# First layer of tiles 3 and 4 one by one from the same sixteen weight buffers, second layer for both; the other tiles in groups of two, two and three

## The chip, the core and the metric

The kernel runs on one core of a Trainium2 chip. The metric is the device time of one execution in microseconds (us). Before the change it took 667.05 us, the median of three runs (666.74 to 670.57).

## What is computed

Attention that keeps the 32 largest scores of each row, then two feed-forward layers. Everything is float32.

```
scores = scale * q @ k.T                     # 2 batches x 8 heads x 576 x 576, head_dim 64
kth = 32nd largest of each row
attn = softmax(where(scores >= kth, scores, -1e9))
x = (attn @ v) of all heads side by side     # 1152 tokens x 512
h = x @ w_in;  g = max(h, 0) + log1p(exp(-|h|));         x = g @ w_out     # 512 -> 2048 -> 512
h = x @ w_in2; g = max(h, 0) + alpha * min(h, 0);   result = g @ w_out2    # 512 -> 2048 -> 512
```

## The kernel before

The 1152 tokens are nine tiles of 128. Attention works on one tile and one head at a time, 72 rows of work in the order of `rows`: tiles 3, 4, 5, 6, 7, 8, 0, 1, 2. For each row TensorE makes the scores (`pss`, L454), ScalarE copies them out (`s`, L459), VectorE finds the 32 largest with four MAX8 and three MATCH_REPLACE8 (L463, L466), ScalarE and GpSimd build the masked exponentials (`e`: L492, L497, L499), TensorE turns them round (`pp`, `pq`: L512, L518), ScalarE copies that (`pt`), and TensorE multiplies by v (`pav`, L540). After the eighth head of a tile, `pr` (L587) spreads the reciprocal sums and the tile's `x` is ready.

The feed-forward part works on groups of tiles (`CHUNKS`, L34): tiles 3 and 4, then 5, 6 and 7, then 8, 0, 1 and 2. For a group, each layer runs over 16 slices `j` of the 2048 hidden columns: `up(j)` makes 128 hidden columns in `ph` (four matrix products of 128 by 128 weights with all tokens of the group), ScalarE and VectorE apply the activation (`g`), `down(j)` multiplies `g` by the output weights into `pa`. The weights of two slices make a unit of 128 x 1024; a layer has 8 units for `up` and 8 for `down`, so both layers have 32.

- The weights come as 64-bit numbers. The first group to need a unit converts it (`convert`): two DMAs into `cr` (one of two buffers, `RAWB`), VectorE L336 and L339, ScalarE L342 twice, GpSimd L345 four times into `cx`, one of the `RING` = 12 buffers called `wring`; a DMA then writes it to scratch memory in DRAM (`ws`).
- The first group (`NATIVE`) multiplies in plain float32, straight from `cx`. The profile shows such a product as two records.
- The other groups fetch the unit from scratch (`w`) and split it (`fetch`): ScalarE casts it to the high part `wh` (L376), GpSimd or VectorE subtracts to get the low part (two halves, `low_piece`, L355 or L356). `x` and `g` are split in the same way (`xh`, `xl`, `gh`, `gl`; `gh` is ScalarE's L662). A product is then three faster matrix products (`three`, L607 to L609).
- In the last group's first layer `down` is turned: the weights are the stationary operand and `g` streams (L608 `pa<-gh,w` is that form's order of names).

The order of all work on all engines is written out by hand in `ORDER`: numbers are operations, a `b` picks the second engine of an operation that has two (VectorE in `low_piece`), and `fN` puts N idle products on TensorE (`scrap`, L766; each one float32 product of 128 x 128, two records in the profile). There are 333 of these. Every engine runs its instructions strictly in this order, so whatever stands behind a waiting instruction on an engine waits with it.

## Time and profile before

| | us | share of the span |
|---|---|---|
| median of three runs | 667.05 | |
| the profiled execution's own time | 665.57 | |
| its span | 663.8 | |
| TensorE (PE) busy | 650.0 | 98% |
| weight loads (PEld) busy | 505.3 | 76% |
| VectorE (DVE) busy | 526.0 | 79% |
| ScalarE (ACT) busy | 487.3 | 73% |
| GpSimd (POOL) busy | 392.6 | 59% |

All times below are from this one profiled execution. Its own time is 1.8 us more than its span, and 1.5 us less than the median of the runs. PE's busy time contains the 333 idle products. A duration given for one instruction reaches a little into the next one of its engine, so rows that follow one another start closer together than their durations say; where that matters, the start-to-start distance is used. [...]

### The profile page before, as it was taken

To read this page: it belongs to the slowest core of one execution; us is meant where nothing else is said; L and a number is where in the kernel's file an instruction comes from. 1 tells how busy PE (TensorE), PEld (TensorE's weight loads), DVE (VectorE), ACT (ScalarE), POOL (GpSimd) and SP (SyncE) were. 2 spreads that over 40 slices of the span, in tenths; PEclk is the share of its full clock that TensorE was granted. 3 is DMA by queue.
4 is the path that set the end of the run, shared out by engine and by line. 5 is a ranking of instruction groups with operands and counts; after the bars stand their busy time and mean duration, and the time that the engine had idled before them with its cause. 6 is when DMAs were issued, how large, how long until landed. Compare 5 with 4: busy or idle time off the path is not lost.

```text
span 663.8 us, 12012 instructions
## 1 busy us (share of the span) xinstructions
PE 650.0 (98%) x4246; PEld 505.3 (76%) x4246; DVE 526.0 (79%) x1003; ACT 487.3 (73%) x1017; POOL 392.6 (59%) x418
## 2 busy tenths in 40 slices
PE   9999999899999999999999999999999999999997
PEld 7789987666656656578887788888888888888885
DVE  4999999999999999999999999899442436434332
ACT  3777777999999888999899886677774647534331
POOL 1466566556875789877878868778632324433310
PEclk9999999999999999999999999999999999999999
DMA  8657466466677688633323112232432223212301
GB/s 294 238 165 244 153 205 227 152 205 192 210 233 240 222 275 265 193 135 112 120 96 112 64 59 76 90 96 64 135 136 95 91 71 125 96 63 98 125 0 63
DMA packets 29579, 96.85 MB, mean 146 GB/s; under 512 B 3408, under 2 KB 3920, under 8 KB 29520
## 3 DMA queue, kind: packets, MB, share of 16 engines
q1 hardware_dynamic: 29520, 96.10, 44.1%
q8 instruction: 33, 0.54, 0.3%
q14 instruction: 26, 0.21, 0.1%
HBM read 76.95 MB, written 19.14 MB: 145 GB/s over the span
## 4 chain that ended last, share of the span: by engine, by line
PE 86%; POOL 4%; ACT 3%; issue 3%; DVE 2%; DMA 1%; SPq 0%; POOLq 0%
PE ph L607 8%; PE pa L607 8%; PE ph L635 8%; PE scrap L766 8%; PE ph L608 8%; PE ph L609 8%; PE pa L609 8%; PE pa L608 8%; PE pa L681 7%; PE pss L454 6%; PE pp L512 4%; POOL cx L345 2%; POOL e L497 2%; DMA cr<-in_w_dram 1%; PE pav__1557 L540 1%
## 5 line engine op out<-in xcount | busy, mean ns | idle before, releaser
L355 POOL TENSOR_TENSOR w<-w,wh 128x512 fp32r<-128x512 f32 x93 | 137.9, 1498 | 110.5 <-ACT wh L376 108.1
L463 DVE MAX8 m<-r 128x8 f32<-128x576 f32 x216 | 155.8, 747 | 0.1
L497 POOL TENSOR_TENSOR e<-s,e 128x288 f32<-128x288 f32 x144 | 120.8, 858 | 56.1 <-ACT e L492 46.2
L345 POOL TENSOR_TENSOR cx<-cx,cr 128x256 int32<-128x256 int32 x128 | 95.1, 766 | 42.3 <-ACT cr L342 38.4
L466 DVE MATCH_REPLACE8 r<-m,r 128x576 f32<-128x576 f32 x144 | 106.2, 741 | 0.0
L342 ACT ACTIVATE cr<-cr 128x512 int16<-128x512 uint32 x64 | 83.8, 1384 | 3.5 <-DVE cr L339 3.4
L766 PEld LDWEIGHTS scrap<-ident 128*128 128x128 f32 x666 | 78.7, 195 | 9.6 <-issue 8.2
L766 PE MATMUL scrap<-ident 128*128 128x128 f32 x666 | 84.0, 282 | 1.4 <-POOL ident masks.py:199 1.4
L376 ACT CAST wh<-w 128x1024 fp32r<-128x1024 f32 x64 | 66.8, 1046 | 15.6 <-DMA w<-ws 14.2
L459 ACT COPY s<-pss 128x288 f32<-128x288 f32 x144 | 53.3, 408 | 24.3 <-PE pss L454 23.6
L607 PE MATMUL pa<-w,gh 128*128 128x512 f32 x160 | 66.6, 416 | 0.0
L463 DVE MAX8 m<-s 128x8 f32<-128x576 f32 x72 | 52.8, 748 | 15.5 <-ACT s L459 14.4
L681 PE MATMUL pa<-cx,g 128*128 128x512 f32 x128 | 63.6, 605 | 0.9 <-POOL cx L345 0.9
L609 PE MATMUL pa<-wh,gh 128*128 128x512 f32 x160 | 63.2, 395 | 0.0
L608 PE MATMUL pa<-wh,gl 128*128 128x512 f32 x160 | 63.1, 395 | 0.0
L499 ACT ACTIVATE e<-e,nb 128x576 f32<-128x576 f32 x72 | 55.7, 774 | 9.9 <-POOL e L497 9.7
L662 ACT CAST gh<-g 128x384 fp32r<-128x384 f32 (+1 forms) x64 | 35.9, 564 | 30.4 <-PE pa L609 19.8
L454 PE MATMUL pss<-ks,q 64*64 64x288 f32 x576 | 51.8, 428 | 2.3 <-ACT pt L515 1.6
L356 DVE TENSOR_TENSOR w<-w,wh 128x512 fp32r<-128x512 f32 x35 | 29.8, 857 | 30.1 <-ACT wh L376 29.9
L466 DVE MATCH_REPLACE8 r<-m,s 128x576 f32<-128x576 f32 x72 | 53.2, 741 | 0.0
L356 DVE TENSOR_TENSOR gl<-g,gh 128x512 fp32r<-128x512 f32 (+1 forms) x36 | 27.5, 764 | 30.9 <-ACT gh L662 30.9
L515 ACT COPY pt<-pp 128x512 f32<-128x512 f32 x72 | 41.5, 587 | 11.2 <-PE pp L512 10.9
(126 smaller groups left out, 1383.0 us busy)
## 6 DMA issues: line engine op xcount, KB each, us to landing
cr<-in_w_dram SPq DMA_DIRECT2D x64, 512.0 KB, 5.3
w<-ws SPq DMA_DIRECT2D x64, 512.0 KB, 3.3
ws<-cx SPq DMA_DIRECT2D x32, 512.0 KB, 6.3
v<-in_v_dram SPq DMA_DIRECT2D x12, 320.0 KB, 6.6
ks<-in_k_dram SPq DMA_DIRECT2D x11, 288.0 KB, 4.3
out_dram<-o SPq DMA_DIRECT2D x9, 256.0 KB, 2.0
q<-in_q_dram SPq DMA_DIRECT2D x8, 256.0 KB, 4.5
ks<-in_k_dram SPq DMA_DIRECT2D x2, 144.0 KB, 2.9
```

Source lines behind the costliest of these rows:

```text
L342: op("ACT", lambda r=r: nc.scalar.activation(r().bitcast(I16)[:, :, 2], r()[:, :, 0], AF.Copy, scale=2.0 ** -29), reads=[part], writes=[r])
L345: op("POOL", lambda part=part, r=r, cs=cs: nc.gpsimd.tensor_add(part().bitcast(I32)[:, cs], part().bitcast(I32)[:, cs], r().bitcast(I32)[: ...
L355: lambda: nc.gpsimd.tensor_sub(lo(), x(), hi().bitcast(F32)),
L454: nc.tensor.matmul(pss[n]()[part], qr()[head, pair, part], ks()[head, cs], start=True, stop=True)
L463: op("DVE", lambda: nc.vector.max(out=out(), in_=x()), reads=reads, writes=writes)
L466: op("DVE", lambda: nc.vector.match_replace(out=out(), in_to_replace=found(), in_values=x(), imm_value=LOWEST), reads=reads, writes=writes)
L497: op("POOL", lambda cs=cs: nc.gpsimd.tensor_sub(e()[:, cs], s()[:, cs], e()[:, cs]), reads=[s], writes=[e])
L607: nc.tensor.matmul(acc, ah, b_l, start=first, stop=False)
L608: nc.tensor.matmul(acc, a_l, bh, start=False, stop=False)
L609: nc.tensor.matmul(acc, ah, bh, start=False, stop=last)
L681: nc.tensor.matmul(acc(), gh()[:, cs], w[0]().bitcast(F32), start=first, stop=last)
L766: plan.emit(ORDER, lambda: nc.tensor.matmul(scrap()[:, :P], ident, ident, start=True, stop=True))
```

## The change

`CHUNKS` becomes five groups: tile 3; tile 4; tiles 5 and 6; tiles 7 and 8; tiles 0, 1 and 2. `TOGETHER` says that the groups of tile 3 and of tile 4 share their second layer, so this layer runs once for 256 tokens, as before. `NATIVE` keeps plain float32 for exactly these two tiles. `RING` goes from 12 to 16 buffers. `lies` remembers which unit lies in which buffer, and `fetch` returns at once where a float32 group finds its unit still there: tile 4's first layer uses the 16 buffers that tile 3's first layer converted. `HOLD` would start a layer at another slice; it is 0 here and moves nothing. `ORDER` is written anew, with 227 idle products instead of 333.

```diff
--- before.py
+++ after.py
@@ -31,8 +31,8 @@
 LOWEST = -3.0e38
 STEEP = 2.0 ** 80
 
-CHUNKS = [[3, 4], [5, 6, 7], [8, 0, 1, 2]]
-TOGETHER = [[0], [1], [2]]
+CHUNKS = [[3], [4], [5, 6], [7, 8], [0, 1, 2]]
+TOGETHER = [[0, 1], [2], [3], [4]]
 SB = 8
 RB = 2
 EB = 2
@@ -46,8 +46,9 @@
 LEAD = 4
 ULEAD = 2
 RAWB = 2
-RING = 12
-NATIVE = {(1, 0), (0, 0)}
+RING = 16
+NATIVE = {(0, 1), (1, 1), (0, 0)}
+HOLD = {(0, 1): 0}
 
 
 class Buffer:
@@ -148,135 +149,157 @@
 
 
 ORDER = """
...
 """
 
 
@@ -320,13 +343,17 @@
     units = [(layer, j, m) for layer in (0, 1) for j in range(FJ // GROUP) for m in (0, 1)]
     ready, scratch = {}, {}
 
-    def slot(tag, bufs, dtype, name):
-        return Halves(buf(tag, bufs, [P, WIDE], dtype, name))
+    lies = {}
+
+    def slot(tag, bufs, dtype, name, unit=None):
+        x = Halves(buf(tag, bufs, [P, WIDE], dtype, name))
+        lies[x.whole.key] = unit
+        return x
 
     def convert(unit):
         layer, j, m = unit
         nm = f"{layer}{m}{j}"
-        f = slot("wring", RING, U32, f"cx{nm}")
+        f = slot("wring", RING, U32, f"cx{nm}", unit)
         raw = Halves(buf("craw", RAWB, [P, WIDE, 2], U32, f"cr{nm}"))
         source = mats[layer][m][j].bitcast(U32)
         for part in raw.parts:
@@ -362,10 +389,12 @@
 
     def fetch(unit, no, ci, whole):
         fresh = unit not in scratch
+        if whole and unit in ready and lies.get(ready[unit][0].whole.key) == unit:
+            return
         if fresh:
             x = convert(unit)
         else:
-            x = slot("wring", RING, F32R, f"w{no}")
+            x = slot("wring", RING, F32R, f"w{no}", unit)
             op("SP", lambda: nc.sync.dma_start(x().bitcast(F32), scratch[unit]),
                reads=["ws%d%d%d" % (unit[0], unit[2], unit[1])], writes=x.parts)
         ready[unit] = (x,)
@@ -622,11 +651,11 @@
             self.turned = layer == 0 and ci == len(CHUNKS) - 1 and len(among[ci]) == 1 and not self.native
             self.g = {}
 
-        def up(self, j):
+        def up(self, j, at):
             n, nm, ci = self.n, f"{self.layer}{self.ci}_{j}", self.ci
             w = [x.parts[j % GROUP] for x in ready[self.layer, j // GROUP, 0]]
             hp = bank("ph", 2, n, f"ph{nm}")
-            step = 1 if j == 0 and self.x[0] is not self.x[-1] else 2
+            step = 1 if at == 0 and self.x[0] is not self.x[-1] else 2
             for c0 in range(0, KT, step):
                 def products(c0=c0):
                     for c in range(c0, c0 + step):
@@ -663,11 +692,11 @@
             low_part(gl, g, gh, n, [g, gh], [gl])
             self.g[j] = gh, gl
 
-        def down(self, j):
+        def down(self, j, at):
             nm, ci = f"{self.layer}{self.ci}", self.ci
             parts_of_g = self.g.pop(j)
             gh, gl = parts_of_g[0], parts_of_g[-1]
-            first, last = j == 0, j == FJ - 1
+            first, last = at == 0, at == FJ - 1
             w = [x.parts[j % GROUP] for x in ready[self.layer, j // GROUP, 1]]
             parts = KT if self.turned else len(self.tiles)
             if first:
@@ -752,14 +781,16 @@
             lay = Layer(layer, ci)
             for j in range(-ULEAD, FJ):
                 if j + ULEAD < FJ:
-                    if (j + ULEAD) % GROUP == 0:
-                        fetch((layer, (j + ULEAD) // GROUP, 0), no, ci, lay.native)
-                    lay.up(j + ULEAD)
+                    n = (j + ULEAD + HOLD.get((layer, ci), 0)) % FJ
+                    if n % GROUP == 0:
+                        fetch((layer, n // GROUP, 0), no, ci, lay.native)
+                    lay.up(n, j + ULEAD)
                     no += 1
                 if j >= 0:
-                    if j % GROUP == 0:
-                        fetch((layer, j // GROUP, 1), no, ci, lay.native)
-                    lay.down(j)
+                    n = (j + HOLD.get((layer, ci), 0)) % FJ
+                    if n % GROUP == 0:
+                        fetch((layer, n // GROUP, 1), no, ci, lay.native)
+                    lay.down(n, j)
                     no += 1
 
     with tc.manual_schedule():
```

The counts in the sections below are of the instructions in program order. A float32 product counts there once, where the profile has two records. What the new order looks like at three places follows; names are those of the code with a running number, and the rows of the changed kernel have its own line numbers.

TensorE from the point where tile 3's attention is done (`pr`), before the change. `scrap` are idle products, `pq` and `pp` turn attention rows round.

```order
L587 MATMUL pr__908<-ident,rx_885 128x128 x4
L766 MATMUL scrap<-ident 128x128 x15
L518 MATMUL pq_943<-ident,e_71 128x128
L512 MATMUL pp_945<-ident,e_71 128x128 x4
L766 MATMUL scrap<-ident 128x128 x7
L540 MATMUL pav__971<-pt_73,v_180 64x64 x10
L540 MATMUL pav__971<-pt_73,v_163 64x64 x10
L766 MATMUL scrap<-ident 128x128 x2
L512 MATMUL pp_1009<-ident,e_72 128x128 x4
L766 MATMUL scrap<-ident 128x128 x15
```

The same place after the change.

```order
L616 MATMUL pr__874<-ident,rx_785 128x128 x4
L797 MATMUL scrap<-ident 128x128 x10
L541 MATMUL pp_906<-ident,e_71 128x128 x4
L797 MATMUL scrap<-ident 128x128 x2
L664 MATMUL ph_1_918<-xh_911,cx_218 128x128 x4
L664 MATMUL ph_0_925<-xh_911,cx_218 128x128 x4
L547 MATMUL pq_939<-ident,e_71 128x128
L541 MATMUL pp_941<-ident,e_71 128x128 x4
L569 MATMUL pav__956<-pt_73,v_167 64x64 x10
L569 MATMUL pav__956<-pt_73,v_171 64x64 x10
L664 MATMUL ph_3_987<-xh_911,cx_272 128x128 x4
L664 MATMUL ph_2_998<-xh_911,cx_272 128x128 x4
```

Behind `pr` stood idle products alone between the attention rows of tile 4; now the first layer of tile 3 (`ph` with 128 columns, weights `cx`) begins there.

TensorE after the change, where the first layer of tile 4 begins. `xh_911` is tile 3's input in the rows above, `xh_1582` is tile 4's; `py` belongs to the end of tile 3's first layer.

```order
L710 MATMUL pa_1024<-cx_1523,g_15_1532 128x512
L664 MATMUL ph_0_1594<-xh_1582,cx_218 128x128 x4
L664 MATMUL ph_1_1607<-xh_1582,cx_218 128x128 x2
L590 MATMUL py_1614<-ident,o_1603 128x128 x4
L664 MATMUL ph_1_1607<-xh_1582,cx_218 128x128 x2
L483 MATMUL pss_1626<-ks_867,q_372 64x288 x2
L483 MATMUL pss_1629<-ks_867,q_372 64x288 x2
L569 MATMUL pav__1639<-pt_73,v_171 64x128 x10
L664 MATMUL ph_2_1658<-xh_1582,cx_272 128x128 x4
L483 MATMUL pss_1669<-ks_867,q_372 64x288 x2
L483 MATMUL pss_1672<-ks_867,q_372 64x288 x2
L710 MATMUL pa_1680<-cx_392,g_0_1612 128x512
```

Tile 4's products name the same buffers `cx_218` and `cx_272` as tile 3's; no conversion and no DMA stands between. The queue of DMAs has no fetch (`w<-ws`) for tile 4: 96 fetches in all, 32 for each of the three later groups, where there were 64.

TensorE where the first three-product layer begins, before the change (tiles 5, 6 and 7) and after it (tiles 5 and 6).

```order
L512 MATMUL pp_3115<-ident,e_71 128x128 x4
L518 MATMUL pq_3120<-ident,e_71 128x128
L607 MATMUL ph_0_3122<-xl_2050,wh_2645 128x384
L608 MATMUL ph_0_3122<-xh_2040,w_2546 128x384
L609 MATMUL ph_0_3122<-xh_2040,wh_2645 128x384
L607 MATMUL ph_0_3122<-xl_2050,wh_2645 128x384
L608 MATMUL ph_0_3122<-xh_2040,w_2546 128x384
```

```order
L541 MATMUL pp_2909<-ident,e_72 128x128 x4
L636 MATMUL ph_0_2919<-xl_2185,wh_2364 128x256
L637 MATMUL ph_0_2919<-xh_2175,w_2291 128x256
L638 MATMUL ph_0_2919<-xh_2175,wh_2364 128x256
L636 MATMUL ph_0_2919<-xl_2185,wh_2364 128x256
L637 MATMUL ph_0_2919<-xh_2175,w_2291 128x256
L638 MATMUL ph_0_2919<-xh_2175,wh_2364 128x256
```

The moving side of a product shrinks from 384 to 256 columns; the number of weight loads for each slice stays at twelve.

## Rows read from the trace of the kernel before

**Rows 1.** Busy time by stretch: columns are stretch, us, then each engine (instructions).

```profile
core 0: us, PE busy (x) PEld busy (x) DVE busy (x) ACT busy (x) POOL busy (x), PEclk, DMA share, GB/s
0.00:54.00 54.00, 52.64 (x480) 44.17 (x481) 44.59 (x89) 36.26 (x78) 22.90 (x36) 1.00 0.71 235
54.00:102.00 48.00, 46.51 (x487) 43.00 (x486) 46.68 (x93) 36.10 (x77) 30.82 (x40) 1.00 0.61 200
152.00:210.00 58.00, 57.42 (x347) 36.56 (x348) 57.55 (x116) 55.94 (x126) 42.39 (x53) 1.00 0.68 219
266.00:317.00 51.00, 48.89 (x332) 35.83 (x331) 49.27 (x101) 47.07 (x110) 40.30 (x43) 1.00 0.47 149
0.00:473.00 473.00, 463.20 (x3426) 354.70 (x3427) 448.16 (x900) 393.29 (x875) 334.15 (x385) 1.00 0.52 169
473.00:663.80 190.80, 186.85 (x823) 150.62 (x821) 77.81 (x104) 93.97 (x142) 58.49 (x34) 1.00 0.26 88
```

**Rows 2.** The last attention rows' transposes on PE: ns min/median/max, first and last start.

```profile
L512 PE MATMUL pp<-ident,e x32: 270/272/273, 440.8 to 473.0; 128*128 128x128 f32 x32
```

**Rows 3.** PE in order of time (start us, us): eleven products of 384, 34 of 512.

```profile
286.28 0.34 PE L608 MATMUL ph<-xh,w 128*128 128x384 f32 x1
...
288.05 0.34 PE L609 MATMUL ph<-xh,wh 128*128 128x384 f32 x1
...
519.22 0.39 PE L608 MATMUL ph<-xh,w 128*128 128x512 f32 x1
...
526.87 0.40 PE L608 MATMUL pa<-gh,w 128*128 128x512 f32 x1
```

**Rows 4.** Chain that ended last, in order of time: start us, us, what, records.

```profile
19.93 5.33 PE scrap L766 x46
...
136.14 0.87 PE pp L512 x8
...
137.88 0.86 PE ph L635 x4
```

**Rows 5.** Groups by form, weight loads: count, busy us, mean ns, idle before.

```profile
L766 PEld LDWEIGHTS scrap<-ident 128*128 128x128 f32 x666 | 78.7, 195 | 9.6 <-issue 8.2 <-POOL ident masks.py:199 1.4
```

**Rows 6.** Groups by form, VectorE.

```profile
L356 DVE TENSOR_TENSOR w<-w,wh 128x512 fp32r<-128x512 f32 x35 | 29.8, 857 | 30.1 <-ACT wh L376 29.9
L655 DVE SCALAR_TENSOR_TENSOR g<-g,rest,ph 128x384 f32<-128x384 f32 x16 | 9.6, 600 | 0.2 <-ACT g L653 0.2
L649 DVE SCALAR_TENSOR_TENSOR g<-ph,g 128x384 f32<-128x384 f32 x16 | 8.7, 543 | 1.1 <-ACT g L648 0.9 <-ACT kb L491 0.3
L655 DVE SCALAR_TENSOR_TENSOR g<-g,rest,ph 128x256 f32<-128x256 f32 x16 | 7.4, 464 | 0.1
L649 DVE SCALAR_TENSOR_TENSOR g<-ph,g 128x256 f32<-128x256 f32 x16 | 6.6, 413 | 0.0
```

**Rows 7.** Groups by form, ScalarE.

```profile
L342 ACT ACTIVATE cr<-cr 128x512 int16<-128x512 uint32 x64 | 83.8, 1384 | 3.5 <-DVE cr L339 3.4
L376 ACT CAST wh<-w 128x1024 fp32r<-128x1024 f32 x64 | 66.8, 1046 | 15.6 <-DMA w<-ws 14.2 <-PE ph L635 1.5
L647 ACT ACTIVATE g<-g 128x384 f32<-128x384 f32 x16 | 8.5, 530 | 0.1
L653 ACT ACTIVATE g<-ph 128x384 f32<-128x384 f32 x16 | 7.8, 488 | 5.4 <-PE ph L609 5.4
L647 ACT ACTIVATE g<-g 128x256 f32<-128x256 f32 x16 | 6.9, 432 | 0.1
L653 ACT ACTIVATE g<-ph 128x256 f32<-128x256 f32 x16 | 6.1, 390 | 0.9 <-PE ph L635 0.8
```

**Rows 8.** ScalarE in order of time: start us, us, instruction.

```profile
162.53 0.48 ACT L647 ACTIVATE g<-g 128x256 f32<-128x256 f32 x1
162.91 0.58 ACT L515 COPY pt<-pp 128x512 f32<-128x512 f32 x1
```

**Rows 9.** Groups by form, GpSimd.

```profile
L355 POOL TENSOR_TENSOR w<-w,wh 128x512 fp32r<-128x512 f32 x93 | 137.9, 1498 | 110.5 <-ACT wh L376 108.1 <-issue 2.3
```

More of the change, by code (lines that the diff above doesn't have):

```diff
@@ new lines @@
+2924 2496 2946 2521 2925b 2856 2911 2872 2533 2873 2857 2494 2534 2956 2858 2910 2878 2933 2859b 2879 2495
+2871 2890 2535 2880 2511 2935b 2934 2947 2891 2881 2888 2970 2536 2949b 2896 2512 2948 2882 2889 2892 2883b
+2957 2509 2897 2510 2537 2902 2893 2982 2959b 2894 2903 2522 2527 2958b 2904 2971 2538 2914 2895b 2915 2973
+2972b 2912 3002 2916 2913 2523 2983 2920 2905 2921 2917 2906 2984b 2985 2918 2926 2524 3014 2907b 2927 2539
+2525 2919 2928 2938 2545 2526 3003 2540 2929 2542 2937 2546 2547 2930 3004b 2541 2950 3005 2543 2945 2931b
@@ new lines @@
+3100b 3101 3040 3050 3142 3041 3052 3042 3054 3043 3131 3053 3044 3133b 3132 3070 3045b 3055 3064 3162 3056
+3062 3143 3065 3057 3082 3145b 3144 3085 3058 3084 3059 3071 3051 3072 3063 3073 3083 3060 3174 3163 3086
+3061b 3074 3164b 3087 3165 3075 3096 3194 3076 3097 3088 3077b 3094 3089 3095 3090 3102 3091 3206 3175 3115
+3092 3116 3176b 3177 3117 3093b 3118 3195 3103 3196b 3197 3114 3104 3129 3207 3119 3105 3209b 3208 3126 3106
+3226 3120 3127 3107 3121 3128 3108 3134 3246 3122 3109b 3123 3135 3124 3125b 3148 3136 3150 3137 3138 3151
@@ new lines @@
+3227 3139 3160 3140 3228b 3264 3229 3152 3149 3141b 3247 3146 3161 3153 3249 3147 3154 3248b 3166 3180 3167
+3155 3156 3158 3265 3157b 3159 3178 3168 3274 3266b 3267 3182 3169 3170 3183 3171 3172 3181 3290 3184 3173b
+3190 3185 3198 3186 3187 3193 3199 3275 3192 3276b 3277 3200 3179 3201 3191 3188 3214 3202 3300 3189b 3291
+3203 3215 3204 3292b 3293 3212 3205b 3316 3216 3210 3217 3211 3218 3213 3219 3225 3220 3222 3221b 3223 3301
+3224 3230 3302b 3326 3303 3232 3234 3317 3236 3238 3231 3318b 3319 3242 3235 3239 3233 3240 3243 3237 3241
@@ L280 @@
+3422b 3423 3356 3348 3360 3349 3431 3350 3372 3432b 3446 3433 3361 3351b 3373 3358 3374 3362 3383 3375 3363
+3385 3364b 3386 3447 3398 3387 3449b 3448 3399 3388 3392 3400 3367 3401 3384 3393 3365 3382 3376 3424 3377b
+3389 3390b 3410 3409 3391 3408 3402 3425 3403b 3411 3426 3427 3412 3418 3413 3417 3414 3415 3434 3416b 3437
+3419 3435 3428 3438 3429b 3444 3439 3451 3440 3436 3443 3441 3445 3442b 3452 3454 3450 3459 3458 3463 3453
+3455 3457 3456 3462 3461 3460 3464
 """
```

125 lines of the change are left out of this document (54 added, 71 removed), and 135 rows, old and new, of the table ORDER.

## The prediction

> **What bounds the kernel now.** I read the busy times by stretch first, then the last attention rows on PE, then PE's instructions in order of time. The last transposes of an attention row start at 473.0 us [rows 2], and that splits the span. Up to there PE (463.2 of 473.0 us) and VectorE (448.2) are both nearly full, ScalarE is at 393.3 and GpSimd at 334.2; behind it PE alone is full, 186.9 of 190.8 us, and the others stand below half [rows 1]. So the end is the time at which attention is through, plus the feed-forward work that PE has left by then. PE's fullness up to 473 us is partly sham: 333 idle products stand there. 46 of their records take 5.33 us [rows 4], 0.116 us each, two for a product: 333 x 0.232 = 77 us.
>
> Distances on PE, start to start: 384 columns (286.28 to 288.05, ten steps) 0.177 us; 512 columns (519.22 to 526.87, 33 steps) 0.232 us [rows 3]. A float32 record of 256 columns takes 0.86 / 4 = 0.215 us [rows 4].
>
> **PE, behind the last attention row.** Before, 795 three-product matmuls of 512 columns stand there in program order: 184.4 us, which with the attention's last pieces and 2% of waits makes the 190.8. After, 180 of 512, 576 of 384 and 30 of 256 columns: 41.8 + 102.0 + 3.7 = 147.5 us. No row shows 256 columns in this form. The line through 384 and 512 falls 0.055 us for each 128 columns, to 0.122. The bounds are 0.116, the pace of the idle products, each of which has a weight load of its own that lasts 195 ns [rows 5] and still keeps that pace, and 0.177, if the pace of 384 is a floor. I take 0.122, since the idle products show that loads follow each other that closely. The tail loses 184.4 - 147.5 = **37 us**: 190.8 becomes 153.8.
>
> **PE, up to the last attention row.** In the same counts 384 matmuls of 384 columns go (-68.0), 738 of 256 come (+90.0), and 87 more of 512 (+20.2). Tiles 3 and 4 one by one turn 64 float32 products of 256 columns into 128 of 128: 64 x 2 x 0.215 = 27.5 us become 128 x 2 x 0.116 = 29.7, the idle product's own shape (+2.2). Four more transposes `py` at 0.109 [rows 4] add 0.4. Together +44.8 us of work, and 106 idle products less give back 106 x 0.232 = 24.6. Net +20 us: with the idle time that PE had, 473 becomes **493**.
>
> **VectorE in the same part.** By program order it gets 13 more weight halves at 0.857 us (+11.1), 24 more pieces L655 of 256 at 0.464 and 14 less of 384 at 0.600 (+2.7), and of L649 32 of 128 (0.283 by the line through 0.413 and 0.543), 16 more of 256, 16 less of 384 (+7.0) [rows 6]. The low parts `gl`, 15 of 256 for 3 of 384 at L649's prices, add 4.5; six masks that go to ScalarE (0.74 by that line) take 4.4. That is 20.9 us in 61 more instructions. Instructions that follow each other start about 0.1 us before the one ahead ends (162.53 + 0.48 against 162.91) [rows 8], so 15 us remain: 448.2 + 15 + the 24.8 it was idle = **488**.
>
> **ScalarE in the same part.** The 32 added unit splits cost 32 casts of 1.046 us (+33.5). Smaller groups mean more pieces: L647 and L648 get 64 of 128 columns at 0.334 (by the line through 0.432 and 0.530; +21.4), 32 more of 256 (+13.8) and 32 less of 384 (-17.0); L646 and L653 32 of 128 at 0.292 (+9.3), 44 more of 256 (+17.2) and 31 less of 384 (-15.1) [rows 7]. The `gh` casts, 60 of 256 for 29 of 384 at L647's prices, add 10.4; six masks and four copies about 7. That is 80.5 us in 188 more instructions, less 0.1 us each: 62 us, so 455. After the first 54 us, in which ScalarE cannot be filled (36.3 us), 419 us are left for it. The fullest stretch of before ran it at 55.94 of 58 us, 96%, with VectorE at 99% and PE at 99%; another, with waits on it, at 47.07 of 51, 92% [rows 1]. At 96% attention ends at 54 + 435 = 489, at 92% at 54 + 454 = 508. The point where ScalarE is tightest is tile 4's attention (54 to 102 us): it had 36.1 us of 48 there, and gets the casts of eight conversions where there were five (6 x 1.384 = +8.3) [rows 7] and 39 pieces of tile 3's first layer (about +9), 53 us in all, so this stretch grows to about 55.
>
> **GpSimd and DMA.** 44 more halves at 1.498 us [rows 9] make 66 us, so 400 of about 495, covered by the same stretch; if it were late, the three products that need the low half would wait, and with them every attention transpose behind on PE. 32 fetches of 512 KB more are 17 MB in about 400 us, beside a DMA share of 0.52 before 473 us [rows 1]; the 16 buffers give a fetch four more to run ahead into. I cost them at nothing; that would fail only if a fetch stood behind a late conversion on the one queue. Tile 4 fetches nothing.
>
> **Sum.** PE says 493, VectorE 488, ScalarE 489 to 508. They are different queues of one order, and each wait of one is felt by the others; I take 495, a little behind the latest of the best cases. 495 + 153.8 = 648.8, 15.0 us under the span of 663.8; taken off the median of 667.05 (the profiled execution itself took 665.57) that is **652 us**.
>
> **Rivals.**
> *ScalarE becomes the bound.* Attention then ends at 508: 508 + 153.8 = 661.8, or 665 for the median. For it: three engines at 94% and more at once, which before held for one stretch only, and conversions that must run through two `cr` buffers faster than before in 54 to 102. Against it: those 58 us show that it can be done. It eats the whole gain at 510 us, that is with ScalarE under 92%.
> *Weight loads set the pace of the short products.* Slower. Twelve loads of 128 x 128 stand before twelve products of 256 columns for each slice, 768 products in all. If their distance stays at 0.177, they cost 768 x 0.055 = 42 us more: 694. The gain is gone from 0.122 + 15 / 768 = 0.142. Against it: the idle products' 0.116. [...]
> *Nothing waits more than before, and VectorE alone sets the pace.* 488 + 153.8 = 641.8: 645. It needs PE to lose some of its 10 idle us.
> *PE's clock falls.* Tile 5's attention loses all idle products and has about 40 us of work in 53. The granted clock was 1.00 throughout, in 54 to 102 with idle products filling [rows 1]. [...]
> *The buffers are not kept* is excluded: the new order names the same `cx` buffers and no fetch.
>
> **Chances.** Forecast, 646 to 660 us: 0.55. ScalarE bound, 660 to 670: 0.2. VectorE alone, 642 to 646: 0.12. Weight loads, 690 and more: 0.06. Clock or something else, 670 to 690: 0.07. About 1%, 6.7 us, is what a measurement can tell from no change: faster than 660.4 is the forecast, the VectorE case and a little of ScalarE's, 0.68; within 1% nearly all of the rest of ScalarE's, 0.2; slower 0.12. The range of 643 to 668 leaves out the lower end of VectorE's case and all above 668, about 0.17.
>
> **What would show it.** Last transposes on PE at 490 to 500 us; a tail of about 154 us; steps of 0.12 us between products of 256 columns; about 454 records of `scrap`; ScalarE at 94% up to the last row; granted clock 1.00. Wrong would make it above all: ScalarE under 92% before the last row, or a step above 0.142.

## The result and the profile after

The changed kernel takes **675.08 us** (median of 7 runs, 672.56 to 679.16), the kernel before 667.33 (7 runs). The ratio is 1.0118, 95% interval 1.0085 to 1.0152: about 1.2% slower, where 652 us and a gain of 2.3% were forecast. The profiled execution took 674.34 us, with a span of 672.6. In the table of runs below, the ratios leave out one slow execution each of one_input and short_topk, and the medians include them.

The last attention row on TensorE splits this span as it split the one before [rows 2] (ns min/median/max, first and last start):

```profile
L541 PE MATMUL pp<-ident,e x32: 270/272/273, 474.6 to 520.4; 128*128 128x128 f32 x32
```

Attention is through at 520.4 us; 495 was forecast, and 473.0 it was before. What stands behind is 672.6 - 520.4 = 152.2 us, forecast 153.8, before 190.8. So the tail came out as worked out, and the whole miss (25 us at the last row) lies ahead of that row. The stretches of [rows 1], now of the changed kernel:

```profile
core 0: us, PE busy (x) PEld busy (x) DVE busy (x) ACT busy (x) POOL busy (x), PEclk, DMA share, GB/s
54.00:102.00 48.00, 45.18 (x425) 34.92 (x424) 48.00 (x104) 43.69 (x105) 32.33 (x43) 1.00 0.68 226
152.00:210.00 58.00, 51.43 (x348) 33.57 (x347) 56.64 (x119) 52.73 (x131) 42.53 (x53) 1.00 0.72 229
266.00:317.00 51.00, 51.00 (x380) 40.66 (x379) 45.30 (x95) 48.20 (x121) 43.55 (x46) 1.00 0.52 167
0.00:520.00 520.00, 492.11 (x3783) 379.67 (x3784) 486.42 (x969) 448.09 (x1060) 402.25 (x446) 0.99 0.57 187
520.00:672.60 152.60, 148.60 (x817) 139.85 (x816) 77.89 (x112) 84.00 (x148) 56.99 (x34) 1.00 0.33 109
```

Up to the last row TensorE is busy for 492.1 us and idle for 27.9, where it was idle for 9.8 before [rows 1]. VectorE is busy for 486.4, ScalarE for 448.1, GpSimd for 402.3. No engine is full from end to end.

Where the attention part lost its time shows in two more views. First, when the float32 products of tiles 3 and 4 run (`xh` is their first layer, `yh` the second). Of the kernel before:

```profile
L635 PE MATMUL ph<-xh,cx x128: 379/379/483, 120.3 to 193.5; 128*128 128x256 f32 x128
L635 PE MATMUL ph<-yh,cx x128: 379/379/483, 203.7 to 268.4; 128*128 128x256 f32 x128
```

Of the changed kernel:

```profile
L664 PE MATMUL ph<-xh,cx x256: 272/275/421, 75.7 to 187.8; 128*128 128x128 f32 x128
L664 PE MATMUL ph<-yh,cx x128: 379/379/634, 195.2 to 261.1; 128*128 128x256 f32 x128
```

Tile 3 alone starts its first layer 44.6 us earlier, and all that is left of it at the end of the second layer is 7.3 us. Second, the exponentials of the attention rows (two records a row) in the kernel before, up to the end of those products and behind it:

```profile
core 0: us, ACT busy (x), PEclk, DMA share, GB/s
0.00:120.30 120.30, 14.48 (x34) 1.00 0.66 218
120.30:268.80 148.50, 19.82 (x46) 1.00 0.68 219
268.80:473.00 204.20, 27.70 (x64) 1.00 0.32 104
```

and in the changed kernel:

```profile
0.00:75.70 75.70, 8.14 (x19) 1.00 0.69 229
75.70:261.50 185.80, 22.61 (x54) 0.98 0.73 235
261.50:520.00 258.50, 31.22 (x72) 0.99 0.43 139
```

Before, 80 records, 40 rows, are through at 268.8 us, 6.7 us a row; now 73 records, 36.5 rows, at 261.5, 7.2 us a row. Behind that a row takes 204.2 / 32 = 6.4 us before and 258.5 / 36 = 7.2 now. The second figure had to rise, since the feed-forward work taken out of the tail stands there. The first had not: by count, the work of tiles 3 and 4 is nearly the same.

### The profile page after: what moved, and what is told of

It reads as the page before. It is cut to its first block, busy times and chain, and to the rows that moved or that the text cites. A ratio compares the mean times of both kernels' runs of the same rounds, so it can differ in the third digit from the quotient of the medians.

```text
span 672.6 us, 13231 instructions
## 1 busy us (share of the span) xinstructions
PE 640.7 (95%) x4598; PEld 519.5 (77%) x4598; DVE 564.3 (84%) x1079; ACT 532.1 (79%) x1207; POOL 459.2 (68%) x480
## 4 chain that ended last, share of the span: by engine, by line
PE 48%; DVE 21%; ACT 10%; issue 8%; POOL 7%; DMA 5%; SPq 0%; POOLq 0%; DVEq 0%; ACTq 0%
DVE m L492 7%; PE ph L636 7%; PE ph L638 7%; PE ph L637 7%; PE pa L636 6%; DVE r L495 6%; PE pa L638 6%; PE pa L637 6%; DMA cr<-in_w_dram 5%; POOL cx L372 4%; PE pss L483 2%; POOL e L526 2%; PE pa L710 2%; DVE cr L366 2%; PE ph L664 2%
## 5 line engine op out<-in xcount | busy, mean ns | idle before, releaser
L382 POOL TENSOR_TENSOR w<-w,wh 128x512 fp32r<-128x512 f32 x138 | 195.8, 1432 | 76.4 <-ACT wh L405 67.1
L526 POOL TENSOR_TENSOR e<-s,e 128x288 f32<-128x288 f32 x144 | 123.2, 873 | 30.2 <-ACT e L521 23.5
L372 POOL TENSOR_TENSOR cx<-cx,cr 128x256 int32<-128x256 int32 x128 | 95.9, 773 | 54.1 <-ACT cr L369 53.7
L405 ACT CAST wh<-w 128x1024 fp32r<-128x1024 f32 x96 | 100.6, 1050 | 1.7 <-POOL gl L382 1.1
L369 ACT ACTIVATE cr<-cr 128x512 int16<-128x512 uint32 x64 | 83.4, 1378 | 10.0 <-DVE cr L366 9.8
L383 DVE TENSOR_TENSOR gl<-g,gh 128x384 fp32r<-128x384 f32 (+1 forms) x52 | 45.1, 868 | 23.9 <-ACT gh L691 23.5
L636 PE MATMUL ph<-xl,wh 128*128 128x256 f32 (+1 forms) x192 | 60.2, 314 | 4.1 <-DVE g L678 4.1
L691 ACT CAST gh<-g 128x256 fp32r<-128x256 f32 (+1 forms) x96 | 42.0, 440 | 27.5 <-DVE g L684 10.9
L636 PE MATMUL ph<-yl,wh 128*128 128x256 f32 (+1 forms) x192 | 58.9, 307 | 1.5 <-DVE yl L597 1.5
L797 PEld LDWEIGHTS scrap<-ident 128*128 128x128 f32 x454 | 54.0, 196 | 6.8 <-issue 5.4
L797 PE MATMUL scrap<-ident 128*128 128x128 f32 x454 | 57.5, 283 | 1.4 <-POOL ident masks.py:199 1.4
L638 PE MATMUL ph<-xh,wh 128*128 128x256 f32 (+1 forms) x192 | 58.1, 303 | 0.0
L637 PE MATMUL ph<-xh,w 128*128 128x256 f32 (+1 forms) x192 | 58.1, 302 | 0.0
```

Of the source, the lines that this page charges most:

```text
L369: op("ACT", lambda r=r: nc.scalar.activation(r().bitcast(I16)[:, :, 2], r()[:, :, 0], AF.Copy, scale=2.0 ** -29), reads=[part], writes=[r])
L372: op("POOL", lambda part=part, r=r, cs=cs: nc.gpsimd.tensor_add(part().bitcast(I32)[:, cs], part().bitcast(I32)[:, cs], r().bitcast(I32)[: ...
L382: lambda: nc.gpsimd.tensor_sub(lo(), x(), hi().bitcast(F32)),
L383: lambda: nc.vector.tensor_sub(lo(), x(), hi().bitcast(F32))),
L405: op("ACT", lambda: nc.scalar.copy(hi(), x().bitcast(F32)), reads=x.parts, writes=hi.parts)
L526: op("POOL", lambda cs=cs: nc.gpsimd.tensor_sub(e()[:, cs], s()[:, cs], e()[:, cs]), reads=[s], writes=[e])
```

## The experiments

Eighteen kernels ran besides the two. Each is given as a ratio to the kernel before on the same chip; "gain" is the difference of two ratios times 667 us, against the changed kernel (675), or, for a kernel made from the one before, against that. An interval is 0.15 to 0.4% wide to each side and a gain against the changed kernel has two of them, so there gains below some 3 us tell little. Line numbers are those of each kernel's own code.

| kernel | median us | ratio (95%) | gain us |
|---|---|---|---|
| changed | 675.08 | 1.0118 (1.0085 to 1.0152) | |
| halves_pool | 683.85 | 1.0227 (1.0186 to 1.0269) | -7.3 |
| one_input | 676.82 | 1.0110 (1.0068 to 1.0152) | 0.5 |
| no_two_input | 671.24 | 1.0051 (1.0022 to 1.0081) | 4.5 |
| short_g | 674.18 | 1.0111 (1.0083 to 1.0138) | 0.5 |
| short_topk | 671.40 | 1.0036 (1.0003 to 1.0070) | 5.5 |
| topk_early | 672.73 | 1.0077 (1.0053 to 1.0100) | 2.7 |
| pe_cut | 661.35 | 0.9909 (0.9880 to 0.9939) | 13.9 |
| pe_topk_late | 666.14 | 0.9972 (0.9941 to 1.0002) | 9.7 |
| all_cut | 664.25 | 0.9940 (0.9915 to 0.9965) | 11.9 |
| cx_first | 663.08 | 0.9938 (0.9909 to 0.9966) | 12.0 |
| cx_both | 661.08 | 0.9903 (0.9878 to 0.9927) | 14.3 |
| after_reordered | 713.39 | 1.0670 (1.0635 to 1.0705) | -36.8 |
| after_order2 | 688.45 | 1.0316 (1.0282 to 1.0351) | -13.2 |
| before_topk | 666.18 | 0.9972 (0.9957 to 0.9987) | 1.9 |
| before_pe_cut | 662.36 | 0.9902 (0.9874 to 0.9929) | 6.5 |
| before_cx_first | 665.99 | 0.9965 (0.9951 to 0.9980) | 2.3 |
| before_reordered | 691.53 | 1.0343 (1.0324 to 1.0363) | -22.9 |
| before_order2 | 682.93 | 1.0233 (1.0216 to 1.0250) | -15.5 |

### VectorE and its collisions with GpSimd

The trace first pointed at VectorE. It was busy for 38 us more ahead of the last row than before, and its low halves with two inputs had grown long. In 20 to 520 us:

```profile
L383 DVE TENSOR_TENSOR w<-w,wh 128x512 fp32r<-128x512 f32 x23 | 25.3, 1105 | 2.1 <-ACT wh L405 2.1
L383 DVE TENSOR_TENSOR gl<-g,gh 128x256 fp32r<-128x256 f32 x18 | 16.3, 908 | 0.6 <-ACT gh L691 0.5
```

The worst of them, in GpSimd's and VectorE's order of time (start us, us):

```profile
315.45 5.05 POOL L382 TENSOR_TENSOR w<-w,wh 128x512 fp32r<-128x512 f32 x4
320.45 0.75 POOL L382 TENSOR_TENSOR xl<-xn,xh 128x256 fp32r<-128x256 f32 x1
321.14 0.74 POOL L382 TENSOR_TENSOR gl<-g,gh 128x256 fp32r<-128x256 f32 x1
321.82 3.75 POOL L382 TENSOR_TENSOR w<-w,wh 128x512 fp32r<-128x512 f32 x3
...
320.79 5.33 DVE L383 TENSOR_TENSOR w<-w,wh 128x512 fp32r<-128x512 f32 x1
```

A half that takes 0.67 us at its fastest took 5.33, to 326.12, just behind the end of GpSimd's row of instructions at 325.57. **halves_pool** gives 33 of the 42 low halves that VectorE makes ahead of the last row to GpSimd (the mark `b` falls; the expectation takes 33 for all of them, but nine stay):

```
- 1419 1706 1699b 1420 1718 ...
+ 1419 1706 1699 1420 1718 ...
```

> The changed kernel, with all 33 low halves that VectorE makes before its last attention row moved to GpSimd; nothing else moves. Theory P: VectorE loses some 40 us of busy time, GpSimd gains 33 times 0.7 to 1.4 us, about 38, and stands at about 440 us of 510; the last transposes come at 500 to 510 us and the time is 655 to 668 us. Theory A: ScalarE's work is untouched, the halves come later on a fuller GpSimd, and the time is 673 to 682 us.

It got slower by 7 us: VectorE lost work, and GpSimd took it at 1.30 us for a half of weights and 0.75 for one of `g`. The collisions did not go: one of the nine halves left on VectorE took 8.57 us. **one_input** leaves the halves on VectorE but gives 32 of them one input, MAX8 for weights and RECIPROCAL for `g`:

```
+            third or (lambda: nc.vector.max(out=lo()[:, :8], in_=x()))),
...
+                    nc.vector.reciprocal(lo()[:, cs], x()[:, cs])
```

> The changed kernel, with 32 of the 33 low halves that VectorE makes before its last attention row replaced by instructions of the same size that read one SBUF tensor and not two: MAX8 over the 512 columns for weights, RECIPROCAL over the 256 for g. The low parts it leaves are therefore not the differences. Theory P (VectorE and GpSimd get in each other's way when VectorE reads two SBUF tensors; in the changed kernel those halves last 0.9 to 1.1 us where 0.4 to 0.7 is the undisturbed length): each of them falls to about 0.4 to 0.7 us, VectorE's busy time up to the last row falls by 15 to 20 us, the last transposes come at about 505 us instead of 520.4, and the time is 655 to 664 us instead of 675. Theory A (ScalarE is too full, VectorE's longer halves only fill its waits): the halves may get shorter, but VectorE then waits, the last transposes stay at 516 to 521 and the time at 671 to 676 us.

Inconclusive: the MAX8 took 0.68 us, but a RECIPROCAL of 128x256 took 1.73 us, longer than the collided half that it was to replace (0.908). **no_two_input** mends this, for all 41 halves of weights and of `g`: those of `g` become a copy on ScalarE.

```
+                      lambda cs=cs: nc.scalar.copy(lo()[:, cs], x()[:, cs]))
```

> The changed kernel, but the 41 low halves with two inputs that VectorE runs before the last attention row are taken away from it: the 23 of weights (128x512, L383) become a MAX8 of one input (0.68 us as measured, into eight columns), the 18 of g (128x256) become a plain copy on ScalarE; those low parts are then wrong, which leaves part of the computation out. VectorE loses 23 x (1.105 - 0.68) + 18 x 0.908 = 26 us, the same amount as with the third strike left out, and ScalarE gains about 7 us. Theory of collisions with GpSimd (two-input instructions of VectorE and GpSimd hold each other up, and such stops stall the queues behind): last transposes 15 to 25 us earlier and the time 650 to 660, much more than the cut strikes gave, and GpSimd's own halves get shorter. Theory of cross waits: the same as the cut strikes gave, 0 to 6 us, 669 to 675.

4.5 us. **short_topk** takes the same amount off VectorE without touching a half: the third strike (MATCH_REPLACE8) of tiles 5 to 8 is left out.

```
-            strike(r, eight(n - 1), s if n == 1 else r, [s if n == 1 else r, m], [r])
+            strike(r, eight(n - 1), s if n == 1 else r, [s if n == 1 else r, m], [r], n == 3 and 5 <= t <= 8)
```

> The changed kernel, but in the 32 rows of tiles 5 to 8 the third of the three strikes of the best eight (L495, MATCH_REPLACE8 and its MATCH_VALUE_LOAD) is left out, so the fourth eight repeats the third: part of the computation is missing. VectorE loses 32 x (0.741 + 0.077) = 26 us before the last row and nothing else changes. Theory VectorE (it is busy for 486 of the 520 us up to the last row, so the last row comes when its amount is through): the last transposes come 20 to 26 us earlier, near 497, and the time is about 652. Theory of cross waits (TensorE, VectorE, ScalarE and GpSimd are each close to full, in queues of a fixed order that wait for each other, so that no one amount is the bound): 0 to 6 us, 669 to 675.

5.5 us. So 26 us less on VectorE are worth about 5 us whether collisions go with them or not: neither its amount nor the collisions account for the miss. **short_g** leaves out ScalarE's Exp and Ln in the first layer of the groups of two:

```
-                op("ACT", lambda: nc.scalar.activation(g(), g(), AF.Exp, scale=-1.0), writes=[g])
...
+                short = ci in (2, 3)
+                op("ACT", lambda: short or nc.scalar.activation(g(), g(), AF.Exp, scale=-1.0), writes=[g])
```

> The changed kernel without the Exp and the Ln in the first layer of the groups of tiles 5, 6 and of 7, 8: 64 ScalarE instructions of 256 columns less, all before the last attention row, about 0.33 us each from start to start, 21 us. g is then max(h, 0) + |h| there. Theory A: the last transposes come 10 to 20 us earlier than 520.4 and the time is 655 to 665 us. Theory P: ScalarE gets idle time, the time falls by 0 to 5 us, to 670 to 675.

Taking 15 to 21 us off ScalarE shows no gain (0.5 us). **topk_early** asks about VectorE where it is fullest, 48.00 of 48 us in tile 4's rows; its edit is that of short_topk with `t in (4, 5)`.

> The changed kernel with the third strike left out in the rows of tiles 4 and 5 alone (16 rows, 13 us of VectorE, between about 60 and 170 us; part of the computation is missing). There VectorE was busy for 48.00 of 48 us in 54 to 102, tile 4's rows took 55.0 us where they took 43.4 before, and TensorE stood idle for VectorE's g. If VectorE's amount is what tile 4's rows wait for: tile 4's last row comes 5 to 7 us earlier (near 112), tile 5's 10 us, and the time falls by 6 to 12 us, 663 to 669. If it is the order of the hand-offs: tile 4's rows end at 116 to 119 and the time falls by 0 to 4, 671 to 675.

```profile
54.00:102.00 48.00, 44.95 (x435) 36.29 (x434) 44.19 (x89) 42.46 (x103) 32.32 (x41) 1.00 0.70 232
```

VectorE is down to 44.19 us, and the rows went through no faster: 26 records of the exponential by 102 us, as in the changed kernel. The gain, 2.7 us of 13, is within the noise. A full engine was not the bound. The cut of short_topk (tiles 5 to 8) in the kernel before, **before_topk**:

> The second control on the kernel before: the third strike of tiles 5 to 8 left out (32 rows, 26 us of VectorE; part of the computation is missing). In the changed kernel this gave about 4 us. If TensorE alone sets the kernel before from 152 us on: 0 to 3 us, 664 to 667. If VectorE shares the bound there: 5 to 12 us, 655 to 662.

1.9 us of 26: VectorE's amount is no bound there either.

### TensorE

**pe_cut** takes out one of three products of the up half in the groups of two:

```
-        nc.tensor.matmul(acc, ah, b_l, start=first, stop=False)
-        nc.tensor.matmul(acc, a_l, bh, start=False, stop=False)
+        short or nc.tensor.matmul(acc, ah, b_l, start=first, stop=False)
+        nc.tensor.matmul(acc, a_l, bh, start=first and short, stop=False)
...
-                                  c == 0, c == KT - 1)
+                                  c == 0, c == KT - 1, ci in (2, 3))
```

> The changed kernel, but in the two groups of two tiles (5, 6 and 7, 8) the first of the three products of the up half (L636, x low part by w high part or y low part) is left out in both layers: 256 products of 256 columns, at their measured step of 0.122 us 31 us of TensorE; part of the computation is missing. Theory TensorE (its 492 busy us up to 520 set the end): the last transposes come 25 to 31 us earlier, near 492, and the time is 645 to 650. Theory of cross waits: 3 to 10 us, 665 to 672.

13.9 us of 31: between the two theories. (The profiled execution of pe_cut, 668.26 us, is the longest of its eight; their median is 661.35.) Behind 266 us TensorE is the engine that counts, as the row of the changed kernel says, and with the cut (second row, of pe_cut) VectorE is the fullest:

```profile
266.00:520.00 254.00, 248.20 (x1913) 202.83 (x1912) 239.40 (x467) 227.82 (x555) 224.01 (x223) 0.99 0.44 142
```

```profile
266.00:520.00 254.00, 236.22 (x1710) 179.97 (x1709) 244.35 (x470) 229.77 (x562) 226.58 (x226) 0.99 0.44 142
```

**pe_topk_late** adds strikes cut in the same stretch (`n == 3 and t in (7, 8, 0, 1, 2)`), and **all_cut** adds to the product the cuts of short_topk and short_g:

> The changed kernel with two cuts in the same stretch: the first product of the up half in the groups of two (256 products, TensorE less 31 us, as in the run that cut it alone) and the third strike of tiles 7, 8, 0, 1 and 2 (40 rows, VectorE less 33 us, nearly all of it behind 266 us, where those products also stand); those parts of the computation are missing. Theory that TensorE and VectorE together fill the stretch from 266 to 520 us (in the run with the product alone cut, VectorE was busy for 197 of the 203 us behind 317): the two cuts give 20 to 28 us, 647 to 655, where the product alone gave about 10. Theory that the order's waits hold it whatever the amounts: as the product alone, 660 to 667.

> The three cuts in one: the third strike of tiles 5 to 8 (VectorE less 26 us), the first product of the up half in the groups of two (TensorE less 31 us), and Exp and Ln of the first layer of the same groups (ScalarE less 15 to 21 us); those parts of the computation are missing. If one engine at a time were the bound and each cut alone only uncovered the next engine, all three together would give 15 to 26 us, for 650 to 660. Theory of cross waits, in the strict sense that the order alone holds the time: still under 12 us, 663 to 672.

9.7 and 11.9 us: no more than the product alone. VectorE fell to 225.41 us in 266 to 514 us in pe_topk_late, and that uncovered nothing. So about half of TensorE's amount pays; what holds the rest, no amount tells. **before_pe_cut** makes the cut in the kernel before (`ci == 1`):

> A control on the kernel before: in its group of three tiles (5, 6, 7) the first of the three products of the up half is left out in both layers, 128 products of 384 columns, at 0.177 us 22.7 us of TensorE, all of them ahead of the last attention row; part of the computation is missing. In the changed kernel the same cut took 31 us off TensorE and 13.7 off the time, 44%. If TensorE sets the attention part of the kernel before (it was idle for 10 of its 473 us, and full from 152 on), the cut pays nearly in full here: 16 to 22 us, 645 to 651, and what the change did was to make other waits set the end. If the share is the same in both (about 10 us, 657), then TensorE counts alike in both and its amount is not what tells them apart.

6.5 us of 22.7, 29%; in the changed kernel it was 45%. The expectation that the kernel before pays in full fell. By these shares TensorE counts more in the changed kernel than before, not less.

### The order

The program's order is a written list, and in **after_reordered** and **before_reordered** a search rewrites it, with the marks `b` in it; nothing else changes.

```
- 4 2 5 3 364 12 363 0 387 95 f11 6 ...
+ 4 2 364 0 5 363 117 387 3 12 77 386 ...
```

> The changed kernel with the same instructions in another order: the list ORDER is rewritten by a search that replays the measured durations of the traces with every wait, buffer and queue, and counts no collisions and no clock changes; nothing else differs (113 low halves marked for VectorE become 119). Theory of cross waits (the amounts would fit, the listed order does not): attention is through 10 to 28 us earlier, last transposes at 492 to 510, the time 648 to 662. Theory of amounts or contention (busy times of TensorE and VectorE, lengthened by collisions, fill the attention part whatever the order): last transposes still at 515 to 520, 668 to 675.

> The control: the kernel before with its list ORDER rewritten in the same way (85 low halves marked for VectorE become 74). If the listed order of the kernel before is near its best, last transposes stay within 10 us of 473 and the time is 657 to 667; if it gains as much as the changed kernel does by its rewriting (10 to 28 us: 640 to 657), then the order was no peculiarity of the change.

Both lost, by 37 and 23 us. In after_reordered VectorE stood still for the weights' loads (us in total, times, longest):

```profile
DVE cx L366 <- DMA cr<-in_w_dram: 35.6, 12, 9.4
```

So a second search counted the transfers, **after_order2** and **before_order2**:

> The changed kernel with the same instructions once more in another order: the replay behind the first rewritten order let transfers land too soon (VectorE then waited 35.6 us for cr<-in_w_dram, as against 8.9 in the changed kernel), so it now takes the transfers one behind the other at 250 GB/s and 3 us from the last byte to the waiter, and 0.35 us for each issue on SP, which brings the replayed times of both first orders and of both rewritten ones to within 3% of the measured. It still counts no clock changes. Theory that the listed order and its transfers, not the amounts, hold the attention part: VectorE waits under 12 us for cr, last transposes at 495 to 512, the time 648 to 664. Theory that collisions and clock take what an order gives: last transposes at 515 or later, 669 to 690.

> The control: the kernel before, its order rewritten by the same replay. If rewriting helps the kernel before as much as the changed one, 648 to 660; if its listed order is near its best, 660 to 670, and what the changed kernel gains by rewriting is its own.

The 250 GB/s, 3 us and 0.35 us of that replay are the author's estimates, set so that its times meet the measured ones. In the changed kernel's trace the shortest issues on SP take 0.32 to 0.33 us, and from issue to landing a load into `cr` takes 5.7 us and a fetch 3.3 (medians), where those estimates give 5.1 for the 512 KB of either.

13 and 16 us lost. The long wait for loads was gone, and VectorE's wait for ScalarE had stayed, in after_order2:

```profile
DVE g L687 <- ACT g L685: 29.6, 15, 5.1
DVE g L681 <- ACT g L680: 22.4, 11, 4.7
```

That is 52 us; the same two waits make 59 us in after_reordered and 35 in the changed kernel.

The same instructions take 675, 688 or 713 us by their order alone, the granted clock being 1.00 in the run of 688. The forecasts of a gain by rewriting fell, and three of the four runs lie outside all ranges on record. after_order2 lies in the range for collisions and clock (669 to 690), but its clock was not low, so that cause isn't shown. The listed orders are better than these replays could tell. And under each of the three pairs of orders the changed kernel is the slower: 1.2%, 3.2% (1.0670 against 1.0343) and 0.8% (1.0316 against 1.0233).

### The conversion of weights

A further candidate is the way of a unit of weights in the first 266 us: load into one of two `cr` buffers, two passes on VectorE, two on ScalarE (L369), four adds on GpSimd (L372), and only then is the buffer free for the next load. **cx_first** leaves out GpSimd's adds for the first layer, **cx_both** for both layers, **before_cx_first** for the first layer in the kernel before:

```
-                op("POOL", lambda part=part, r=r, cs=cs: nc.gpsimd.tensor_add(
+                op("POOL", lambda part=part, r=r, cs=cs, short=layer == 0: short or nc.gpsimd.tensor_add(
```

> The changed kernel with GpSimd's adds of the conversion (L372, four of 0.72 us for a unit of weights) left out for the 16 units of the first layer, which leaves the low bits of those weights out. GpSimd loses 64 x 0.72 = 46 us between 20 and about 160 us, where it was busy for two thirds of the time, so its amount is not at issue; what gets shorter is the conversion's chain of load (5.7 us), VectorE, ScalarE and GpSimd through two cr buffers, which the chain of waits shows in tile 4's rows (POOL cx 20%, DMA cr 12% of the stretch where early strikes were left out). If that chain holds the rows in which tiles 3 and 4 go through their first layer (row 40 ends at 288.5 us, where it ended at 268.5 before): tile 4's last row at 108 to 114 instead of 118.4, row 40 at 272 to 282, the time 658 to 668. If not: tile 4's last row at 116 to 119 and the time 671 to 676.

> The same for all 32 units, both layers (GpSimd less 92 us, all ahead of 270 us). Theory of the conversion's chain: row 40 ends 12 to 20 us earlier, at 268 to 276, and the time is 650 to 662. Otherwise 668 to 675.

> The control: the kernel before with the adds of the first layer's 16 units left out. If the conversion's chain holds its first 268 us too (its chain of waits shows POOL cx 22% and DMA cr 13% in 63 to 112), it gains 5 to 12 us, 655 to 662; if the chain binds only where tile 3's layer comes at once, 0 to 3 us, 664 to 667.

12.0 us of 46 in the changed kernel, 14.3 of 92 for both layers, and 2.3 in the kernel before, from the engine with the most room: GpSimd was busy for 32.33 of 48 us in 54 to 102. The float32 products of cx_first:

```profile
L664 PE MATMUL ph<-xh,cx x256: 272/275/377, 75.8 to 181.9; 128*128 128x128 f32 x128
L664 PE MATMUL ph<-yh,cx x128: 379/379/483, 189.3 to 252.4; 128*128 128x256 f32 x128
```

They start where they started (75.8) and end 8.7 us earlier than in the changed kernel (261.1). VectorE's wait for loads (us in total, times, longest), first the changed kernel, then cx_first, is halved; the kernel before had 1.7:

```profile
DVE cx L363 <- DMA cr<-in_w_dram: 8.9, 7, 3.5
```

```profile
DVE cx L363 <- DMA cr<-in_w_dram: 4.7, 5, 1.4
```

Not all of the 12.0 is shown to be the adds' own. The last attention row of cx_first starts its last transposes at 506.9 us, 13.5 earlier than in the changed kernel, while 8.7 had come by the end of the layers of tiles 3 and 4. Up to 506 us TensorE was idle for 18.6 us (27.9 in the changed kernel up to 520) and busy for 487.4 (492.1), though nothing was taken off it; the granted clock was 1.00 (0.99):

```profile
0.00:506.00 506.00, 487.43 (x3778) 375.66 (x3779) 479.38 (x967) 446.50 (x1059) 357.07 (x382) 1.00 0.58 191
```

The price on record for the total (658 to 668) was met; that of tile 4's own rows was not, which ended 2.7 us earlier and not 4 to 10. Whether the adds cost their time through the `cr` buffers, as the shorter wait for loads suggests, or by standing ahead of attention's own subtractions (`e`, L526) in GpSimd's queue, these runs don't separate. A third `cr` buffer was not tried.

## Why the prediction was wrong, point by point

**The tail: right.** 152.2 us for 153.8, a loss of 38.6 us for 37.

**The step of 256 columns: right.** In order of time on TensorE, 22 steps:

```profile
292.94 0.28 PE L637 MATMUL ph<-xh,w 128*128 128x256 f32 x1
...
295.53 0.28 PE L638 MATMUL ph<-xh,wh 128*128 128x256 f32 x1
```

2.59 / 22 = 0.118 us, taken as 0.122, and the rival of the weight loads (0.177, 694 us) is out. Each of these products has a weight load of its own, of 0.19 us, and the loads start 0.118 us apart too (2.60 / 22), beside the products:

```profile
292.82 0.19 PEld L637 LDWEIGHTS ph<-xh,w 128*128 128x128 f32 x1
...
295.42 0.19 PEld L638 LDWEIGHTS ph<-xh,wh 128*128 128x128 f32 x1
```

**The sum of TensorE up to the last row: this is the step that failed**, and in it the words "106 idle products less give back 106 x 0.232 = 24.6. Net +20 us: with the idle time that PE had, 473 becomes 493". The products did go:

```profile
L797 PE MATMUL scrap<-ident 128*128 128x128 f32 x454 | 57.5, 283 | 1.4 <-POOL ident masks.py:199 1.4
```

But they gave no time back. They stood in the first 120 us, in which TensorE was not the bound; they filled its waits. [Rows 1] has the sign of it: in 54 to 102 us VectorE was at 46.68 of 48 us, and of TensorE's 46.51 most were filler, as the `scrap` records alone show in that stretch of the kernel before:

```profile
54.00:102.00 48.00, 34.48 (x290) 33.04 (x289) 1.00 0.61 200
```

TensorE could give time back only where it was what the others waited for. In place of the filler came 18 us of true idle time (27.9 against 9.8), and 8.7 us more work than the 483.4 that the sum has (492.1): 18.1 + 8.7 = 26.8, which is the step from 493 to 520. The split at 266 us shows where, first the kernel before, then the changed one:

```profile
0.00:266.00 266.00, 259.01 (x1993) 192.57 (x1994) 253.97 (x510) 220.14 (x475) 170.77 (x220) 1.00 0.67 220
266.00:473.00 207.00, 204.19 (x1435) 162.13 (x1434) 194.18 (x391) 173.15 (x401) 163.38 (x166) 1.00 0.32 105
```

```profile
0.00:266.00 266.00, 243.91 (x1872) 176.84 (x1873) 247.02 (x503) 220.27 (x506) 178.25 (x223) 0.99 0.70 229
```

In the first 266 us TensorE's idle time rose from 7.0 to 22.1 us, 15.1 of the 18.1. What TensorE still had to do then, up to the last row, was 248.2 us of work against 204.2: 44.0 more, where the sum has 42.2 more for the products that stand there (90.0 + 20.2 - 68.0). So at 266 us the changed kernel was no further than the kernel before; the 22 us by which the sum has it ahead (24.6 less 2.6) are missing there. Behind 266 us, 44.0 us more work took 47.0 us more time: there the sum by TensorE's work holds for work that is added. For work taken out it is not safe even there: the products of before_pe_cut stand behind 266 us too, and leaving them out gave 29% of their time. No run took idle products alone out of the kernel before, or put them back into the changed one, which would be the direct test.

**What paced the first part instead.** The prediction costed GpSimd and the transfers at nothing since their amounts fit, and amounts were right (402 us, forecast 400). Yet leaving out GpSimd's adds for one layer gave 12.0 us, and only 2.3 in the kernel before. One thing that differs is how far the conversion is when the first layer begins. VectorE's first pass (one for a unit) up to that time and during the layer, first the kernel before, then the changed one:

```profile
0.00:120.30 120.30, 9.50 (x12) 1.00 0.66 218
120.30:193.50 73.20, 6.92 (x9) 1.00 0.62 196
```

```profile
0.00:75.70 75.70, 6.12 (x8) 1.00 0.69 229
75.70:187.80 112.10, 11.37 (x15) 0.98 0.70 224
```

Before, 12 of the layer's 16 units had had this pass when it began; now 8, and the conversions come at much the same pace, one in 112.1 / 15 = 7.5 us (8.1 before). So tile 3 goes at the pace at which the other eight come: its 64 float32 products of the up half (128 records) fill 17.45 of the 54.3 us from 75.7 to 130.

```profile
75.70:130.00 54.30, 17.45 (x128) 1.00 0.79 256
```

At its end the chain shows itself: the adds of the up half's last unit end at 119.53 us, and the first products that read it start 0.3 us later.

```profile
117.40 2.13 POOL L372 TENSOR_TENSOR cx<-cx,cr 128x256 int32<-128x256 int32 x3
119.84 1.06 PE L664 MATMUL ph<-xh,cx 128*128 128x128 f32 x8
```

In the kernel before, the same unit was through at 141.9 us and its products started at 185.9. How much of the missing 22 us this chain holds is not shown; with the first layer's adds left out, 8.7 us came back by the end of the second layer.

By busy time in 54 to 102 us VectorE, at 48.00 of 48 us, would come far ahead of GpSimd, at 32.33, 67%. The runs do not bear that out, nor the reverse: 13 us less of VectorE gave 2.7, 46 us less of GpSimd gave 12.0, about a fifth and a quarter.

**VectorE: mis-sized, but not the cause.** Forecast were 15 us more ahead of the last row, measured 38.3. The halves are 42 us for 9.5 before: 18 more of weights where 13 were counted, and longer ones, 1.105 and 0.908 us for 0.857 and 0.413 in the sum. Taking 26 us away gave 5.

**ScalarE: the count right (448 us, forecast 455), the rival wrong.** It stands at 448.1 / 520 = 86%, which the prediction named as what would make it wrong above all. ScalarE's fullness did not cause the miss; its cut gave 0.5 us.

**TensorE's clock: a part of it.** The rival had it fall through tile 5's 40 us of work, the author's estimate. The changed kernel's trace does not show that: it shows short falls right behind idle stretches. TensorE waits 4.11 us for VectorE (first row), which the half of 5.33 us had held up, and the mean granted clock of the next 4 us falls to 0.59 of full speed, with 0.50 in 329 to 332 us:

```profile
328.83 0.58 PE L636 MATMUL ph<-xl,wh 128*128 128x256 f32 x1 [4.11 <-DVE g L678]
```

```profile
324.00:328.00 4.00, 0.72 (x4) 0.24 (x2) 4.00 (x5) 0.37 (x3) 1.57 (x2) 1.00 0.69 238
328.00:332.00 4.00, 3.17 (x15) 3.17 (x16) 4.00 (x11) 2.82 (x9) 1.96 (x3) 0.59 0.01 2
329.00:332.00 3.00, 3.00 (x15) 3.00 (x16) 3.00 (x8) 1.82 (x6) 1.96 (x3) 0.50 0.00 0
```

Two more such falls (0.89 to 0.90 in 128 to 144 us, 0.79 in 256 to 264) also follow idle stretches, of 2.8 us each. The mean granted clock over the runs of one kernel goes roughly with their time. Of the changed kernel, spans of 670.8 and 672.6 us had 0.992, two of 675.7 had 0.986 and 0.987 (the longest, 677.4, had 0.989); of cx_first, 659.1 and 659.9 had 0.999 and 1.000, two of 664.7 had 0.991 and 0.992. That is about 5 us for 0.8%, so of the 25 us missed some 5 are the clock's (an estimate from these spans), and the falls seen follow idle time. The band from 670 to 690, in which the result came, had been given a chance of 0.07.

**What stays open.** Why half or more of TensorE's cut is lost, in either kernel, and what wait takes the place of each that goes. Which waits hold the rest of the first 266 us: VectorE's and TensorE's cuts too gave more in the changed kernel than in the one before (5.5 us against 1.9 for 26, and 45% against 29% of the amount), so the adds are not alone in it. One part of the change that no run takes by itself is that tile 4 holds all 16 buffers: the first pass of the second layer's first unit starts at 139.3 us, 12.1 behind the one ahead of it, and VectorE waits for TensorE's use of the buffer there (1.06 us). The other half of the change, groups of two, was not run without tiles 3 and 4 one by one: it needs a list of its own, and lists alone were worth 13 to 37 us here. No run that does the whole computation beat the kernel before.

## What to carry to other kernels

Filler and idle time on an engine are worth something only in stretches where that engine is what others wait for: split the sum by stretch, and in each write down which wait ends last, before work that is taken out is booked as time. Work on an engine far from full can still cost time, through what waits for it, when a change makes its consumer start earlier; price such a chain as latency too, not as amount alone. Where an order is written out by hand for one set of durations, expect a large cut on one engine to give back a fraction (here 2 to 45%), and a new order may cost more than the change can bring.

## What the runs showed of the hardware

- A VectorE half with two inputs that began at 320.79 us ended only behind five of GpSimd's instructions, after 5.33 us, where the shortest of its kind took 0.67. GpSimd's instructions follow each other without a gap there (from 320.45, 321.14 and 321.82 to 325.57 us), and the half did not end between them. Of the halves beside which GpSimd ran nothing, one of 128x512 (at 405.06 us) took 0.67 us and one of 128x256 (at 512.42) 0.41.
- A RECIPROCAL of 128x256 on VectorE took 1.73 us, a MAX8 of 128x512 0.68 (one_input).
- Products of 256 columns, each with its own weight load of 0.19 us, follow each other at 0.118 us, as the idle products of 128 columns do at 0.116 [rows 4].
